# Attention chunks on array quarters: scores and values' products without the masked quarter, in two phases, in a fused gated-attention and expert kernel

## The chip, the cores and the metric

The kernel is one program on one core of a Trainium2 chip. Its time is device time in microseconds (us) from the start to the end of one execution; the time before is the median of three such runs. Beside it stands one execution taken with the hardware profiler. The engines are named as the profile names them: PE is the matrix engine (PEld its weight loads), DVE, ACT and POOL are the three elementwise engines, SP issues most transfers. All data are 32-bit floats; a matmul of the program in that type shows as two passes in the profile's counts (a step's 8 score matmuls are `x16` there), a transpose by the identity as one.

## The reference

Gated linear attention, then a mixture of experts with one expert for each token:

```python
state = np.zeros((B, H, D, D))                       # B=4, H=8, S=768, D=48
for t in range(S):
    state = alpha[:, :, t, :, None] * state + np.einsum('bhd,bhe->bhde', k[:, :, t], v[:, :, t])
    y[:, :, t] = np.einsum('bhd,bhde->bhe', q[:, :, t], state)
x = y.transpose(0, 2, 1, 3).reshape(B * S, H * D)    # 3072 tokens x 384
logits = x @ w_gate + modality_bias[modality_id]     # 8 experts
e = argmax(logits); g = softmax(logits)[e]
out[t] = g * (relu(x[t] @ w1[e]) @ w2[e])            # w1 384x1024, w2 1024x384
```

## The kernel before, in words

**Attention.** A batch's 768 tokens are cut in six chunks of 128, so there are 24 units of work, unit i being chunk i % 6 of batch i // 6, with all 8 heads. Heads go in pairs: pair j holds head 2j on partitions 0 to 47 and head 2j+1 on partitions 64 to 111. For a unit the decays a are turned by PE transposes (`turn_decay`, then two DVE scans in `decay`), k and q are turned and scaled by them (`scale_k`, `scale_q`), and then

- `scores`: kh x qh, 128 keys by 128 queries for each head. ACT copies each of the two results out of PSUM (`scT`), and POOL's affine select sets the entries to zero in which the key lies behind the query.
- `keys`: kh turned back, for the state (`knat`).
- `combine`: one PSUM tile `y` takes three groups of products. U x qh is the state's part of the output (not in a batch's first chunk); kn x v is the state's update (not in the last chunk); v x scT is the chunk's own part. DVE then forms the next state `S` from `y`, and `UB` from it.
- `outputs`, `rows`, `logits_turned`, `logits`: ACT copies y to `yt`, PE turns it into token rows (`xs`, written to DRAM `xd`), and the gate's logits are formed for two units at a time, in every odd step.

The units are pipelined over steps: step s turns the decays of unit s, scales k and q of s-1, does keys and scores of s-2, combine of s-3, outputs and rows of s-4. PE keeps the order in which the program writes its matmuls in steps after the third (`pin`); the other engines' orders come from a scheduler. Step s issues the loads of unit s+2. `guard` is an ACT pass over a unit's decays as they were loaded (`junk`, with a sum `gacc` from which the kernel knows whether a decay is out of range); it stands on ACT ahead of the copy `X` of the same unit's turned decays, and it waits there for the load.

**Experts.** Tokens are ranked by expert and gathered in 12 full slots of 256 tokens and a half slot of 128 (number NS0 = 12). A slot's first layer and second layer each split their operands in a high and a low part and sum three products, `layer1` and `layer2`. `layer2` works for two halves u of 128 tokens; each has a PSUM tile `sc` of its own (two buffers), which ACT scales by the gate into `os`, and POOL scatters `os` to the output (`put`). Before the gather is ready, PE does the first slot's first layer (`first_layer`) with attention steps still running. After the half slot comes a branch on POOL and other engines, on whether more slots are needed; with these inputs none are. The half slot's result is put into `of`, which is scattered behind that branch, at the program's very end.

Of the kernel before, what the change touches and what calls it, by code (L numbers as in the profile page):

```python
# [40 lines left out]
PAD = 32  # L41
# [13 lines left out]
def attention_moe(ctx: ExitStack, tc: tile.TileContext, q, k, v, alpha, mid, wg, mb, w1, w2, out):  # L55
# [12 lines left out]

    def row(i):
        return i * P + (i * P >= MID)  # L70
# [13 lines left out]
    for i in range(NV):  # L84
        t = ac.tile([P, H, 64], F32, name=f"vt{i}")
        VT.append(t)
        pool.memset(t[:, :, D:], 0.0)

# [16 lines left out]
    def first_layer(j, z, name="tr", bufs=3):  # L105

        if z == 0:
            hps.append(ps.tile([P, 2, T], F32, name=name, bufs=bufs))
# [4 lines left out]
    def first_inputs():  # L113
        for d0, d1 in ((0, 2), (2, 3)):
            xp = ps.tile([P, d1 - d0, T], F32, name="sc", bufs=2)
# [23 lines left out]
    for g in range(2):  # L139
        for o in range(2):  # L140
            sp.dma_start(
                wgp[64 * g : 64 * g + D, o::2, :E], wg.rearrange("(a o g d) e -> o g d a e", o=2, g=2, d=D)[o, g ^ o]
            )
# [126 lines left out]

    def scores(i):
        kh, qh = st[i, "k"], st[i, "q"]
        pp = [ps.tile([P, NP, P], F32, name="sc", bufs=2) for _ in range(2)]
        for j in range(NP):
            for g in range(2):
                r = slice(64 * g, 64 * g + D)
                pin(pe.matmul(pp[g][:, j], kh[r, j], qh[r, j], start=True, stop=True))
        st[i, "s"] = []
        for g in range(2):
            s = sb.tile([P, NP, P], F32, name="scT", bufs=4)  # L280
            mark["sc"] = act.copy(s, pp[g])  # L281
            pool.affine_select(s, s, [[0, NP], [1, P]], ALU.is_ge, 0.0, base=0, channel_multiplier=-1)  # L282
            st[i, "s"].append(s)
# [11 lines left out]

    def combine(i):
        c = i % NC
        qh, vt, sc = st[i, "q"], VT[i % NV], st[i, "s"]
        U = UB[i % 2]
        halves = [slice(64 * g, 64 * g + 64) for g in range(2)]  # L300
# [5 lines left out]
        yk = ps.tile([P, 2, 512], F32, name="y")  # L306

        def y(r, j):
            return yk[r, j % 2, P * (j // 2) : P * (j // 2 + 1)]

        kv = yk[:, 1, 2 * P : 2 * P + NP * D].rearrange("p (j d) -> p j d", j=NP)
        fresh = {(o, g) for o in range(2) for g in range(2)}

        def first(o, g):
            new = (o, g) in fresh
            fresh.discard((o, g))
            return new

        if c > 0:
            for a in range(2):  # L320
                for o in range(2):
                    for g in range(2):
                        x, j = g ^ o, 2 * a + o
                        pin(pe.matmul(y(halves[x], j), U[halves[g], j], qh[halves[g], j], start=first(o, x), stop=False))
        if c < NC - 1:
            kn = st[i, "n"]
            for h in range(H):
                j = h // 2
                r = halves[h % 2]
                pin(pe.matmul(kv[r, j], kn[:, j, r], vt[:, h, :D], start=first(1, h % 2), stop=False))  # L330
        for j in range(NP):
            for x, r in enumerate(halves):
                g = x ^ j % 2
                pin(pe.matmul(y(r, j), vt[:, 2 * j + g], sc[g][:, j], start=first(j % 2, x), stop=(j > 1)))
        if c < NC - 1:
            S1 = sb.tile([P, NP, D], F32, name="S")
            if c > 0:
                vec.tensor_tensor(S1, U[:, :, :D], kv, op=ALU.add)
            else:
                vec.tensor_copy(S1, kv)  # L340
# [3 lines left out]
    def outputs(i):  # L344
        yt = sb.tile([P, 2, NP, P], F32, name="yt") if i % 2 == 0 else st[i - 1, "yt"]
        with issue_after("X"):
            act.copy(
# [449 lines left out]
    for s in range(NU + 3):  # L797
# [28 lines left out]
        if s < NU:  # L826
            guard(s)
# [257 lines left out]
```

## Time and profile before

| what | value |
|---|---|
| median of 3 runs | 405.47 us (403.87 to 410.87) |
| profiled execution | 406.9 us, of it a span of 405.2 us |
| mean granted clock of PE in it | 0.983 |
| busy: PE, DVE, ACT, POOL | 378.9, 272.8, 224.1, 136.0 us |
| steady attention steps | 25.6 to 126.2 us of the span, 17 steps |
| end of attention, routing | to about 178 us |
| expert slots | 178 to 398 us |

Times in the profile's rows are counted from the start of the span. A row of the timeline has the start and the length of a run of like instructions on an engine, both in us, then the line of the program, the operation, output and inputs, how much of the array a matmul uses (rows by columns), and, in brackets, how long the engine stood idle before and what ended that. The next run on the same engine may begin before the last has ended, since the engines are pipelined; the distance from start to start is what a run costs.

### The profile page before, as it was taken

How to read it: one execution, taken by the hardware profiler on the slowest of the kernel's cores; microseconds unless marked ns; L12 is line 12 of the kernel's file. 1: busy time of each engine (PE TensorE's matmuls, PEld its weight loads, DVE VectorE, ACT ScalarE, POOL GpSimd, SP SyncE). 2: the span in 40 equal slices, each digit the busy share in tenths (PEclk: the TensorE clock that was granted, in tenths of full speed). 3: DMA queues.
4: the chain of work that ended last, by engine and by line, in shares of the span. 5: the costliest groups of instructions: out<-in, count | busy, mean ns of one | idle time of the engine just before them, and what ended most of it. 6: DMA issues, size and time to landing. Idle time of an engine off the chain costs nothing. (4 is left out here: it accounts for less than half of the span.)

```text
span 405.2 us, 9558 instructions
## 1 busy us (share of the span) xinstructions
PE 378.9 (94%) x3659; PEld 349.0 (86%) x3659; DVE 272.8 (67%) x550; ACT 224.1 (55%) x425; POOL 136.0 (34%) x175
## 2 busy tenths in 40 slices
PE   3898999999999987989997999999999999999992
PEld 3787788888878776779997999999999999999992
DVE  6787889878889962487688566665756666554230
ACT  3467577567665543345586646565554656545230
POOL 9321311321233253302665515344251634222010
PEclk9999999999999997999998999999999999999998
DMA  6999898678764079505999776576867657520010
GB/s 127 202 199 224 195 196 174 149 169 194 152 156 109 21 255 344 183 22 195 387 356 345 250 260 209 201 229 191 278 190 261 212 197 241 147 104 35 6 42 10
DMA packets 132655, 75.12 MB, mean 185 GB/s; under 512 B 103777, under 2 KB 120222, under 8 KB 132600
## 3 DMA queue, kind: packets, MB, share of 16 engines
q1 hardware_dynamic: 128504, 64.57, 56.9%
q0 software_dynamic: 4096, 9.85, 7.1%
q8 instruction: 31, 0.51, 0.5%
q14 instruction: 24, 0.20, 0.1%
HBM read 64.95 MB, written 9.65 MB: 184 GB/s over the span
## 5 line engine op out<-in xcount | busy, mean ns | idle before, releaser
L925 PE MATMUL tr<-xH,w1H 128*128 128x256 f32 x264 | 74.7, 286 | 1.3 <-DVE hL L932 1.3
L926 PE MATMUL tr<-xL,w1H 128*128 128x256 f32 x264 | 75.0, 285 | 0.0
L927 PE MATMUL tr<-xH,w1L 128*128 128x256 f32 x264 | 74.9, 285 | 0.0
L282 POOL TENSOR_SCALAR_AFFINE_SELECT scT<-scT 128x512 f32<-128x512 f32 x48 | 35.6, 763 | 102.3 <-ACT scT L281 102.3
L948 PE MATMUL sc<-w2H,hH 128*128 128x384 f32 x192 | 65.3, 342 | 1.0 <-ACT hH L929 1.0
L949 PE MATMUL sc<-w2L,hH 128*128 128x384 f32 x192 | 64.4, 336 | 0.0
L950 PE MATMUL sc<-w2H,hL 128*128 128x384 f32 x192 | 63.5, 340 | 0.0
L899 DVE TENSOR_TENSOR w2L<-w2r,w2H 128x768 fp32r<-128x768 f32 x52 | 49.1, 957 | 20.5 <-ACT w2H L897 20.3
L899 DVE TENSOR_TENSOR w1L<-w1r,w1H 128x768 fp32r<-128x768 f32 x44 | 41.7, 956 | 21.2 <-ACT w1H L897 20.6
L866 POOL DMA_INDIRECT out_dram<-os,odx x24 | 26.8, 1116 | 83.8 <-ACT os L953 35.6
L897 ACT CAST w1H<-w1r 128x768 fp32r<-128x768 f32 x44 | 36.0, 834 | 29.8 <-PE tr L926 22.9
L925 PEld LDWEIGHTS tr<-xH,w1H 128*128 128x128 f32 x264 | 50.9, 194 | 1.6 <-issue 1.6
L926 PEld LDWEIGHTS tr<-xL,w1H 128*128 128x128 f32 x264 | 51.2, 194 | 0.0
L927 PEld LDWEIGHTS tr<-xH,w1L 128*128 128x128 f32 x264 | 51.0, 194 | 0.0
L679 POOL DMA_INDIRECT xg<-xd,idx x26 | 31.3, 1206 | 50.7 <-PE y L887 41.6
L897 ACT CAST w2H<-w2r 128x768 fp32r<-128x768 f32 x52 | 42.2, 835 | 6.9 <-PE sc L950 6.8
L932 DVE SCALAR_TENSOR_TENSOR hL<-tr,hH 128x512 fp32r<-128x512 f32 x46 | 31.5, 685 | 10.4 <-ACT hH L929 7.9
L948 PEld LDWEIGHTS sc<-w2H,hH 128*128 128x128 f32 x192 | 36.1, 188 | 2.4 <-ACT hH L929 1.2
L684 POOL DMA_INDIRECT gg<-gd,idx x26 | 30.6, 1177 | 17.4 <-DMA gd<-gs 10.1
L949 PEld LDWEIGHTS sc<-w2L,hH 128*128 128x128 f32 x192 | 36.1, 188 | 0.0
L950 PEld LDWEIGHTS sc<-w2H,hL 128*128 128x128 f32 x192 | 36.0, 188 | 0.0
L929 ACT ACTIVATE hH<-tr 128x512 fp32r<-128x512 f32 x46 | 27.3, 593 | 15.3 <-PE tr L927 9.5
(218 smaller groups left out, 702.3 us busy)
## 6 DMA issues: line engine op xcount, KB each, us to landing
w1r<-in_moe_w_dram SPq DMA_DIRECT2D x26, 768.0 KB
w2r<-in_moe_w_dram SPq DMA_DIRECT2D x26, 768.0 KB
nat_a<-in_alpha_dram SPq DMA_DIRECT2D x24, 192.0 KB
nat_k<-in_k_dram SPq DMA_DIRECT2D x24, 192.0 KB
nat_q<-in_q_dram SPq DMA_DIRECT2D x24, 192.0 KB
vt<-in_v_dram SPq DMA_DIRECT2D x24, 192.0 KB
xd<-xs SPq DMA_DIRECT2D x24, 192.0 KB
xg<-xd,idx POOLq DMA_INDIRECT x26
```

Of the source, the lines that this page charges most:

```text
L282: pool.affine_select(s, s, [[0, NP], [1, P]], ALU.is_ge, 0.0, base=0, channel_multiplier=-1)
L679: pool.indirect_dma_start(xg[i % NX][:, u], None, xd[0:rows], ix, bounds_check=rows - 1, oob_is_err=False)
L684: pool.indirect_dma_start(gg[i % NX][:, u : u + 1], None, gd[0:rows], ix, bounds_check=rows - 1, oob_is_err=False)
L897: act.copy(hi, src)
L899: vec.tensor_tensor(lw, src, hi.bitcast(F32), op=ALU.subtract)
L925: pe.matmul(hp[:, z], wH[:, d, fs], xH[:, d], start=(d == 0), stop=False)
L926: pe.matmul(hp[:, z], wH[:, d, fs], xL[:, d], start=False, stop=False)
L927: pe.matmul(hp[:, z], wL[:, d, fs], xH[:, d], start=False, stop=(d == ND - 1))
L932: mark[f"h{j}L"] = vec.scalar_tensor_tensor(hL, hp, 0.0, hH.bitcast(F32), op0=ALU.max, op1=ALU.subtract)
L948: pe.matmul(op, hH[:, z, us], wH[:, z], start=(f == 0), stop=False)
L949: pe.matmul(op, hH[:, z, us], wL[:, z], start=False, stop=False)
L950: pe.matmul(op, hL[:, z, us], wH[:, z], start=False, stop=(f == NF - 1))
```

## The change

1. `scores` does 16 matmuls where there were 8. Each takes 64 keys of one head on a 64x64 quarter of the array. For the second 64 keys only the second 64 queries are computed, since the first 64 are masked (the batch's very first unit computes all, so that the rest of the tile is never unset). The two banks of one lasting PSUM tile `banks` take the results; POOL masks only the 64x64 diagonal blocks, in four selects instead of two of 128x512.
2. `combine` is cut in two phases, as a generator. The state's update and the values' products go 64 keys at a time on quarters, half of them in phase 0, half in phase 1. Between the phases stand the next unit's scores. Phase 1's first matmul waits for a memset of one element on POOL (`tick`), which itself waits for the last matmul of phase 0. Half of the heads' values are needed on the other half of the partitions as well: two POOL copies for each unit (`VS`).
3. `bank(n)` hands out the two halves of `banks` by turns, where a pool of two `sc` tiles was before: in `first_layer`, `first_inputs`, `layer2`, `half`.
4. The half slot's result goes into an ordinary `os`, and its `put` stands in `half`, in front of the last branch; `of` and its memset are not used for it any more.
5. `first_layer(0, ...)` is written around the two phases of step 25's combine, the gate's weights and the copies out of `y` follow the new places of the heads (same sizes), and a filler tile is 24 columns wide instead of 32.

```diff
     def scores(i):
+
         kh, qh = st[i, "k"], st[i, "q"]
-        pp = [ps.tile([P, NP, P], F32, name="sc", bufs=2) for _ in range(2)]
-        for j in range(NP):
-            for g in range(2):
-                r = slice(64 * g, 64 * g + D)
-                pin(pe.matmul(pp[g][:, j], kh[r, j], qh[r, j], start=True, stop=True))
-        st[i, "s"] = []
-        for g in range(2):
-            s = sb.tile([P, NP, P], F32, name="scT", bufs=4)
-            mark["sc"] = act.copy(s, pp[g])
-            pool.affine_select(s, s, [[0, NP], [1, P]], ALU.is_ge, 0.0, base=0, channel_multiplier=-1)
-            st[i, "s"].append(s)
+        pp = banks.rearrange("p g (a o t) -> p g a o t", a=2, o=2)
+        for o in range(2):
+            for z in range(2):
+                for a in range(2):
+                    for g in range(2):
+                        j, r, t = 2 * a + o, slice(64 * g, 64 * g + D), slice(64 * z if i else 0, P)
+                        ins = pe.matmul(pp[halves[z ^ a], g, a, o, t], kh[r, j, halves[z]], qh[r, j, t], start=True, stop=True)
+                        pin(ins)
+        s = sb.tile([P, 2, 2, 2, P], F32, name="scT")
+        for a in range(2):
+            mark["sc"] = act.copy(s[:, a], pp[:, :, a])
+            for b in range(2):
+                m = s[halves[b], a].rearrange("p g o t -> p (g o) t")[:, :, halves[b ^ a]]
+                pool.affine_select(m, m, [[0, 4], [1, 64]], ALU.is_ge, 0.0, base=0, channel_multiplier=-1)
+        st[i, "s"] = s
+        for b in range(2):
+            pool.tensor_copy(VS[i % 2][halves[b], :, :D], VT[i % NV][halves[1 - b], H // 2 :, :D])
...
+        def phase(n):
+            if n:
+                gate.append(chain(pool.memset(tick, 0.0), done[-1], mybir.DependencyClass.Sync))
+            if c > 0 and n == 0:
+                for a in range(2):
+                    for o in range(2):
+                        for g in range(2):
+                            j = 2 * a + o
+                            part(g, o, P * a, P * (a + 1), U[halves[g], j], qh[halves[g], j])
+            if c < NC - 1:
+                kn = st[i, "n"]
+                for a in range(2):
+                    for o in range(2):
+                        for g in range(2):
+                            j, r, lo = 2 * a + o, halves[o ^ n], 2 * P + D * a
+                            part(o, g, lo, lo + D, kn[r, j, halves[g]], vt[r, 2 * j + g, :D])
             for a in range(2):
...
+                for g in (a, 1 - a):
+                    for o in range(2):
+                        r, z = halves[g ^ n], g ^ n ^ a
+                        h = 4 * a + 2 * o + g
+                        v = vs[r, h - H // 2] if a else vt[r, h]
+                        cuts = (0, 64, P) if n and z == 0 and c == 0 else (64 * z, P)
+                        for lo, hi in zip(cuts, cuts[1:]):
+                            last = n == 1 and a == 1 and hi == P
+                            part(g, o, P * a + lo, P * a + hi, v, sc[r, a, g, o, lo:hi], stop=last)
+
+        phase(0)
+        yield
+        phase(1)
...
-            op = ps.tile([P, DM], F32, name="sc", bufs=2)
+            op = bank(DM)
...
-            late = i == NS0 and u == 0
-            os = of if late else mp3.tile([P, DM], F32, name="os", bufs=4)
+            os = mp3.tile([P, DM], F32, name="os", bufs=4)
             act.activation(os, op, AF.Copy, scale=g[:, u : u + 1])
-            if not late:
-                put(i, u, os)
+            put(i, u, os)
...
-        os = of if i == NS0 else mp3.tile([P, DM], F32, name="os", bufs=4)
+        os = mp3.tile([P, DM], F32, name="os", bufs=4)
         act.activation(os, op, AF.Copy, scale=g[:, 0:1])
-        if i != NS0:
-            put(i, 0, os)
+        put(i, 0, os)
...
         tail(NS0)
-    put(NS0, 0, of)
```

**PE, one odd steady step.** Lines have moved with the change: transposes L227 are now L243, rows L357 are L403, scores L277 are L298, the products of `combine` L324, L330 and L334 are all L343. Before, the step's PE order was:

```order
L227 MATMUL tr<-ident,nat_a_94 128x128 x4
L227 MATMUL tr<-ident,nat_k_90 128x128 x4
L227 MATMUL tr<-ident,nat_q_92 128x128 x4
L291 MATMUL tr<-ident,kh 128x128 x4
L369 MATMUL rt<-yt,wgp 32x256 x4
L357 MATMUL tr<-ident,yt 128x128 x4
L277 MATMUL sc<-qh,kh 128x128 x8
L324 MATMUL y<-qh,UB_154 64x128 x8
L330 MATMUL y<-vt_104,knat 64x48 x8
L334 MATMUL y<-scT,vt_104 64x128 x8
```

In a changed step, from the U products on (the three other rows of phase 1's values follow the last one shown):

```order
L343 MATMUL y<-qh,UB_159 64x128 x8
L343 MATMUL y<-vt_109,knat 64x48 x8
L343 MATMUL y<-scT,vt_109 64x128 x2
L343 MATMUL y<-scT,vt_109 64x64 x2
L343 MATMUL y<-scT,vs_113 64x128 x2
L343 MATMUL y<-scT,vs_113 64x64 x2
L298 MATMUL sc<-qh,kh 64x128 x4
L298 MATMUL sc<-qh,kh 64x64 x4
L298 MATMUL sc<-qh,kh 64x128 x4
L298 MATMUL sc<-qh,kh 64x64 x4
L343 MATMUL y<-vt_109,knat 64x48 x8
L343 MATMUL y<-scT,vt_109 64x64 x2
```

The scores have gone from in front of the U products to between the phases, and 32 matmuls have become 56.

**ACT, the same kind of step.** From one copy `yt` to the next, before, with the guard `junk` behind the two copies `xs`:

```order
L347 COPY yt<-y 128x2x2x128
L293 COPY knat<-tr 128x512
L371 COPY lts<-rt 128x256
L361 COPY xs<-tr 128x2x96
L362 COPY xs<-tr 128x2x96
L250 ACTIVATE junk,gacc<-nat_a_94,bhi 128x384
L281 COPY scT<-sc 128x512 x2
L232 COPY X_150<-tr 128x4x128
```

And in the changed kernel (guard L266, knat L318, lts L417, xs L408, scT L302, X L248):

```order
L396 COPY yt<-y 128x512
L266 ACTIVATE junk,gacc<-nat_a_95,bhi 128x384
L318 COPY knat<-tr 128x512
L417 COPY lts<-rt 128x256
L408 COPY xs<-tr 128x4x48 x2
L302 COPY scT<-sc 128x512 x2
L248 COPY X_155<-tr 128x4x128
```

The guard stands behind `yt` directly, ahead of knat, lts, xs, scT and X. It does so in ten of the sixteen steps from step 8 to 23 (10, 11, 14 to 17, 20 to 23); before, it stood behind `yt` in one of these (step 9).

**PE, the second expert slot.** Before, the end of the second layer, its two PSUM tiles sc_3202 and sc_3232 (u = 0 and 1) taken by turns, then the next slot's first layer:

```order
L948 MATMUL sc_3202<-w2H_3162,hH_3158 128x384 [waits Activation_49]
L949 MATMUL sc_3232<-w2L_3137,hH_3131 128x384
L950 MATMUL sc_3232<-w2H_3135,hL_3133 128x384
L948 MATMUL sc_3232<-w2H_3135,hH_3131 128x384
L949 MATMUL sc_3202<-w2L_3164,hH_3158 128x384 [waits DVE_49]
L950 MATMUL sc_3202<-w2H_3162,hL_3160 128x384
```

In the changed kernel, the end of u = 0, three matmuls of the next slot's first layer, and the start of u = 1:

```order
L996 MATMUL sc_71<-w2L_3771,hH_3765 128x384
L997 MATMUL sc_71<-w2H_3769,hL_3767 128x384
L972 MATMUL tr_3883<-xH0_3519,w1H_3867 128x256 [waits Activation_49]
L972 MATMUL tr_3910<-xH0_3519,w1H_3871 128x256 [waits PE_49]
L972 MATMUL tr_3937<-xH0_3519,w1H_3875 128x256 [waits PE_49]
L995 MATMUL sc_71<-w2H_3688,hH_3684 128x384 [waits Activation_49]
```

Both u write the one tile sc_71, and u = 1 starts behind a wait for ACT, whose instruction is the copy `os` of u = 0.

On POOL, the branch L1036 stood ahead of the last scatter L866 of `of`; now the scatter of `os` (L913) stands ahead of the load and branch (L1079, L1080).

More of the change, by code (lines that the diff above doesn't have):

```diff
@@ L39 @@
 NG = 2 * E
-PAD = 32
+PAD = 24
 EARLY = (16, 18)
@@ L67, in attention_moe, with bank @@
     ps = ctx.enter_context(tc.tile_pool(name="ps", bufs=1, space=PSUM))
+    banks = ps.tile([P, 2, 512], F32, name="sc")
+    turn = []
+    def bank(n):
+        turn.append(n)
+        return banks[:, len(turn) % 2, :n]
     def row(i):
@@ L87, in attention_moe @@
         pool.memset(t[:, :, D:], 0.0)
+    VS = []
+    for i in range(2):
+        t = ac.tile([P, NP, 64], F32, name=f"vs{i}")
+        VS.append(t)
+        pool.memset(t[:, :, D:], 0.0)
     WR = [
@@ L294, in keys, with chain @@
             st[i, "n"] = kn
+    tick = cp.tile([1, 1], F32, name="tick")
+    def chain(ins, other, kind):
+        info = mybir.DependencyInfo(kind, mybir.DependencyReason.DATA)
+        tc.add_manual_dep(ins.ins, other.ins.name, info, reason="row tiles")
+        return ins
     def combine(i):
         c = i % NC
-        qh, vt, sc = st[i, "q"], VT[i % NV], st[i, "s"]
+        qh, vt, vs, sc = st[i, "q"], VT[i % NV], VS[i % 2], st[i, "s"]
         U = UB[i % 2]
-        halves = [slice(64 * g, 64 * g + 64) for g in range(2)]
         if c > 0:
@@ L306, in combine @@
         yk = ps.tile([P, 2, 512], F32, name="y")
[L308 to L319, printed above, removed]
-            for a in range(2):
[L321 to L334, printed above, removed]
+        fresh = {(b, x) for b in range(2) for x in range(2)}
@@ new lines, in combine, with part @@
+        done, gate = [], []
+        def part(b, x, lo, hi, *operands, stop=False):
+            ins = pin(pe.matmul(yk[halves[x], b, lo:hi], *operands, start=(b, x) in fresh, stop=stop))
+            fresh.discard((b, x))
+            if done:
+                chain(ins, done[-1], mybir.DependencyClass.NoSync)
+            if gate:
+                chain(ins, gate.pop(), mybir.DependencyClass.Sync)
+            done.append(ins)
+        def phase(n):
[14 more added lines that the diff above has]
+                            part(o, g, lo, lo + D, kn[r, j, halves[g]], vt[r, 2 * j + g, :D])
+            for a in range(2):
+                for g in (a, 1 - a):
[7 more added lines that the diff above has]
+                            part(g, o, P * a + lo, P * a + hi, v, sc[r, a, g, o, lo:hi], stop=last)
@@ L823, in attention_moe @@
             rows(s - 4)
+        steps = combine(s - 3) if 0 <= s - 3 < NU else iter(())
+        if s == NU + 2:
+            first_layer(0, 0, own=True)
+        next(steps, None)
         if 0 <= s - 2 < NU:
             scores(s - 2)
+        if s == NU + 2:
+            first_layer(0, 1)
+        next(steps, None)
         if s < NU:
@@ L847, in attention_moe @@
     outputs(NU - 1)
-    first_layer(1, 0, "sc", 2)
+    first_layer(1, 0, own=True)
     first_layer(1, 1)
```

41 lines of the change are left out of this document (20 added, 21 removed).

## Prediction

> **What bounds the kernel now.** I read the page's head first: which engine has no air, and when.
>
> ```profile
> PE 378.9 (94%) x3659; PEld 349.0 (86%) x3659; DVE 272.8 (67%) x550; ACT 224.1 (55%) x425; POOL 136.0 (34%) x175
> PE   3898999999999987989997999999999999999992
> ```
>
> PE is busy for 94% of the span, with small holes at the start and around slices 15 to 21. So PE's work counts first. But 94% is an average over two programs, attention and experts, and nearly all of the change lies in attention. The busy times by stage (columns: window, its length, then busy time and count for PE, PEld, DVE, ACT, POOL, then granted clock, DMA share, GB/s):
>
> ```profile
> 25.60:126.20 100.60, 98.17 (x1425) 81.84 (x1426) 85.10 (x178) 67.52 (x161) 24.69 (x34) 1.00 0.83 179
> 126.20:137.00 10.80, 10.80 (x161) 8.80 (x160) 10.41 (x27) 6.57 (x15) 3.01 (x4) 1.00 0.21 58
> 137.00:178.00 41.00, 36.35 (x406) 29.25 (x406) 23.41 (x102) 17.45 (x39) 13.66 (x15) 0.92 0.58 199
> ```
>
> The first row is 17 steady steps, 5.92 us each: PE stands for 2.43 us in all, DVE is at 85%, the transfers at 83%. PE bounds these steps, but the next limits are near, at 85.1 and 83.5 us of 100.6. Third, the timeline of PE for one odd step:
>
> ```profile
> 78.41 0.65 PE L227 MATMUL tr<-ident,nat_a 128*128 128x128 f32 x4
> 78.90 0.60 PE L227 MATMUL tr<-ident,nat_k 128*128 128x128 f32 x4
> 79.34 0.60 PE L227 MATMUL tr<-ident,nat_q 128*128 128x128 f32 x4
> 80.23 0.64 PE L369 MATMUL rt<-yt,wgp 128*32 128x256 f32 x8 [0.29 <-ACT yt L347]
> 80.80 0.66 PE L357 MATMUL tr<-ident,yt 128*128 128x128 f32 x4
> 81.39 1.16 PE L277 MATMUL sc<-qh,kh 48*128 48x128 f32 x16
> 82.48 0.67 PE L324 MATMUL y<-qh,UB 64*64 64x128 f32 x16
> 83.07 0.67 PE L330 MATMUL y<-vt,knat 128*64 128x48 f32 x16
> 83.58 1.06 PE L334 MATMUL y<-scT,vt 128*64 128x128 f32 x16
> 84.56 0.33 PE L227 MATMUL tr<-ident,nat_a 128*128 128x128 f32 x1
> ```
>
> From start to start: scores 1.09, U products 0.59, state 0.51, values 0.98, together **3.17 us** of this step's 6.15. These four are what the change rewrites.
>
> **What it saves on PE, step by step.** A 128-column transpose pass costs 0.11 us (78.90 to 79.34, four of them). The 16 U passes on 64x64 quarters run four side by side: four groups of 0.11 make 0.44, and 0.15 is left for the change of array mode at the block's start. The state's 16 passes, 48 columns wide, two side by side, take 0.51/8 = 0.064 us a pair: so a narrow pass has a floor near 0.06 where its columns would ask for 0.11 x 48/128 = 0.04. The changed block, with four quarters side by side:
>
> - U products as now, 0.59.
> - State: twice as many passes (32), eight groups of four at the floor 0.064: 0.51, as now. The other two quarters come free, and the phases halve the keys.
> - Scores: four groups of 128 columns at 0.11 and four of 64 columns at 0.064: 0.70.
> - Values: eight groups. In a group two quarters have 128 columns and two have 64. In lockstep each costs 0.11: 0.88. If quarters run on their own, nearer 0.70.
>
> The sum is 2.68 us; the scores' and values' own changes of mode (about 0.2 and 0.1 in the old rows) fall away, since the whole block stays in one mode. It saves **0.5 us a step**, 0.7 at best.
>
> Nothing on PE's path grows by the new gate, I think. Phase 1's first matmul waits for a one-element memset on POOL, and that for phase 0's last matmul; the 16 score matmuls, 0.70 us, are issued between. A memset of a [128,1] tile is the nearest row; from a matmul's start to the start of what waits for it I take 0.4 us, worked out from the expert stage's rows below (370.38 to 370.75). So 0.4 + 0.09 + about 0.1 for the signal back: 0.6 under a cover of 0.70. The bounds are 0 and, with the cover gone, 0.6 us a step.
>
> ```profile
> L493 POOL MEMSET beg<- 128x1 f32 x1 | 0.1, 88 | 0.0
> L282 POOL TENSOR_SCALAR_AFFINE_SELECT scT<-scT 128x512 f32<-128x512 f32 x34 | 24.7, 749 | 78.2 <-ACT scT L281 78.2
> ```
>
> Behind the memset on POOL stand the next selects and value swaps, and behind those the values' products of the next step. POOL's load goes from two selects of 0.75 us to four smaller selects, two copies and a memset: by the rows between 0.09 and 0.75 each I take 0.4, 0.35 and 0.09, 2.4 us of a step of over 5. POOL idled for 78.2 us on `scT`, so this hides; if selects stayed at 0.75, 3.8 us would still fit, but the scores' masks would come 1.5 us later, still a step ahead of their use.
>
> **What is late next: ACT.** A saved 0.5 us counts only if `yt` is ready for PE sooner. ACT's order decides it. Before, in a step from 84.56 on (the last PE row is the next step's start):
>
> ```profile
> 89.85 0.65 PE L227 MATMUL tr<-ident,nat_a 128*128 128x128 f32 x4
> ...
> 86.59 0.59 ACT L293 COPY knat<-tr 128x512 f32<-128x512 f32 x1 [0.26 <-PE tr L291]
> 87.25 0.32 ACT L361 COPY xs<-tr 128x192 f32<-128x192 f32 x1
> 87.46 0.33 ACT L362 COPY xs<-tr 128x192 f32<-128x192 f32 x1
> 88.87 0.62 ACT L250 ACTIVATE junk<-nat_a,bhi 128x384 f32<-128x384 uint32 x1 [1.08 <-DMA nat_a<-in_alpha_dram]
> 89.48 1.06 ACT L281 COPY scT<-sc 128x512 f32<-128x512 f32 x2
> 90.55 0.58 ACT L232 COPY X<-tr 128x512 f32<-128x512 f32 x1
> 91.03 0.59 ACT L347 COPY yt<-y 128x512 f32<-128x512 f32 x1
> ...
> 92.48 0.37 ACT L371 COPY lts<-rt 128x256 f32<-128x256 f32 x1
> ...
> 93.66 0.62 ACT L250 ACTIVATE junk<-nat_a,bhi 128x384 f32<-128x384 uint32 x1
> ```
>
> The guard `junk` stands idle until its load lands at 88.87, 4.3 us after the step's start. In the next step, which PE begins at 89.85, it starts at 93.66 without a wait, so there the load had landed within 3.8 us. By the order rows the changed kernel puts the guard right behind `yt` in ten of sixteen steps, ahead of knat, lts, xs, scT and X. From the landing on ACT then does guard 0.6, knat 0.55, xs 0.5, scT 1.05, X 0.5 and the next yt 0.6, in odd steps lts 0.3 as well: the next `yt` is done 3.8 or 4.1 us behind the landing, in an even step 7.6 to 8.1 us after its start.
>
> An odd step needs `yt` for L369 1.82 us after its own start (78.41 to 80.23), an even step about 2.0 for L357 (16 turns of a, k, q and kh and two of logits stand ahead, 18 x 0.11). An odd step is 6.15 us in the rows above and the mean 5.92, so an even one is 5.7; with 0.5 less it is 5.2. It offers 5.2 + 1.82 = 7.0 us up to that use, `yt` comes at 7.6 to 8.1, and the odd step waits for 0.6 to 1.1. A pair of steps gains 1.0 on PE and keeps 0 to 0.4 of it. The even step behind has air again: its use comes some 6.15 + 2.0 = 8.15 us after the odd step's start, and `yt` 7.9 at the early landing. I take **0.3 us** for a pair whose even step has the early guard, and the full 1.0 for the others. The ends are 0 and 1.0 for all. That an early wait of ACT does stop PE is in this trace already, where the guard stood right ahead of X:
>
> ```profile
> 43.06 0.62 ACT L250 ACTIVATE junk<-nat_a,bhi 128x384 f32<-128x384 uint32 x1 [1.23 <-DMA nat_a<-in_alpha_dram]
> 45.01 0.64 PE L369 MATMUL rt<-yt,wgp 128*32 128x256 f32 x8 [0.56 <-ACT yt L347]
> ```
>
> Five even steps have an early guard (10, 14, 16, 20, 22); I give them five of the 8.5 pairs.
>
> **Experts and tail.** Both halves u of `layer2` now share one tile, so u = 1 waits for the copy `os` of u = 0:
>
> ```profile
> 370.38 0.33 PE L950 MATMUL sc<-w2H,hL 128*128 128x384 f32 x1
> 370.67 0.28 PE L926 MATMUL tr<-xL,w1H 128*128 128x256 f32 x1
> 370.75 0.58 ACT L953 ACTIVATE os<-sc,gg 128x384 f32<-128x384 f32 x1 [0.16 <-PE sc L950]
> ```
>
> From the last matmul's start to the end of `os` are 0.95 us, 0.78 of them beyond the matmul's own slot of 0.17. The order fills them with 15 or more first-layer matmuls of 0.12 us (370.55 to 370.67 is one) in most slots, 1.8 us: covered. The first slot has only a few short matmuls there, the second three, 0.36 us: about 0.4 and 0.5 us show, **+0.9**. Without any filler it would be 0.8 x 12 = +9.4.
>
> At the end, the last matmul, the half slot's copy and its scatter, and the chain's row that lies between:
>
> ```profile
> 397.57 0.34 PE L993 MATMUL sc<-w2H,hL 128*128 128x384 f32 x1
> 397.95 0.58 ACT L995 ACTIVATE of<-sc,gg 128x384 f32<-128x384 f32 x1 [3.57 <-PE sc L993]
> 401.38 0.98 POOL L866 DMA_INDIRECT out_dram<-of,odx  x1 [11.12 <-ACTq L1036]
> ```
> ```profile
> 398.27 2.88 issue
> ```
>
> `of` is done at 398.53, the scatter starts 2.85 us later, behind POOL's load and branch, and the span ends 3.8 us after that. Moved ahead, the scatter starts at 398.6; POOL's load and branch still follow it: 398.6 + 1.0 + 2.9 = 402.5, and about 1.3 to close (an estimate: of the 3.8 us now, about 2.5 taken for the scatter's landing). The end is then near 403.8: **-1.4 us**, with bounds 0.5 and 2.85.
>
> **The sum**, against the profiled execution of 406.9 (span 405.2 and 1.7 around it): steady steps -(5 x 0.3 + 3.5 x 1.0) = -5.0; two steps in the second window, where PE is busy throughout, -1.0; the other five units, at the start and in the third window, where PE stands for 4.65 of 41 us, half of 5 x 0.5, -1.3; experts +0.9; tail -1.4. Together -7.8, so 399.1. That execution lies 1.4 above the median of the runs shown, 405.47, so I forecast **397.7**.
>
> **A rule of the Trainium skill against the row.** The floor of a narrow pass decides whether narrower pieces pay. The trace has 0.064 us for the state's 48 columns. The Trainium skill, "TensorEngine Tiling (Array Packing)", section Instruction Overhead, says that a matmul on this chip carries some 60 cycles of overhead, that one with a free size of 1 takes as long as one of 60, and that no tiling factor should be taken from a size that is small already. That speaks against 64- and 48-column pieces. At 0.11 us for 128 columns, its 60 columns are an estimate of 0.052 us; the block by that would be 2.68 less 12 x 0.012, some 2.5 us, so the rule, true as far as the state's row shows, still leaves a gain here, because quarters share the floor four at a time.
>
> **The rivals.**
>
> *All of PE's saving shows* (17%). Loads land earlier, or ACT's wait is absorbed: 24 units at 0.5 to 0.7 is 12 to 16.8, with -1.4 and +0.9 a time of 389.6 to 394.4, by the median 388 to 393. For it: ACT has 33 of 100.6 us idle. Against it: DVE's 85.1/17 = 5.0 us a step against the 5.4 then left, and the order rows.
>
> *No gain in attention* (25%). Either the landing moves back as steps shorten (transfers at 0.83 would need 0.9 of the shorter step; at 4.7 us the pair is as long as now), or quarters don't start independently and every pass costs PE some time of its own however narrow. One full-array row bounds that (the tile's view: shortest, median and longest in ns, first and last start in us):
>
> ```profile
> L632 PE MATMUL rt<-OH,OL x24: 177/177/192, 188.4 to 189.0; 128*128 128x34 f16 x24
> ```
>
> Its 24 passes, 34 columns wide, start within 0.6 us, 26 ns apart (22 to 30 by the rounding). The block grows from 64 to 112 passes; at 26 ns they take 2.9 us and 0.15 for the mode, 3.05: a gain of 0.1 a step, at most 2.5 in all. The time is 404 to 406.4, by the median 402.5 to 405.
>
> *Slower, by passes* (7%). If a quarter pass costs what the U row gives in all, 0.59/16 = 37 ns, then 112 of them cost 4.1 us, 1.0 more than now: +24 us less 0.5, a time of 429. It decides from 3.17/112 = 28 ns on. Against it speak the 26 ns, and that 0.15 of the U row is a one-time cost.
>
> *Slower, by the gate* (6%). If POOL answers phase 1 only after two selects of 0.75, in 2.1 us instead of 0.6, PE stands 2.1 - 0.7 = 1.4 in each of 24 steps and saves 0.5: +21.6, with tail and experts a time of 428. It decides from an answer of 1.2 us on, the cover and the saving together. Against it: POOL's order has the memset ahead of the next unit's selects, and POOL is idle most of a step.
>
> *The forecast* (45%) has 394 to 401 as its own range.
>
> **The numbers.** Two per cent of 405.47, about what a measurement of this kernel tells from no change, is 8.1: faster means under 397.4, slower over 413.6. The forecast lies on the bound, and I put 0.28 of its 0.45 below it. Faster: 0.28 + 0.17 = 0.45. Slower: 0.07 and half of the gate's case, 0.10. Same: the rest, 0.45. The range from 389 to 406 takes in the forecast, the no-gain case and most of the full saving; it leaves out both slower cases and a few chances at either end. What could move any case by 3 us is the granted clock, 0.92 in the third window, if its slow stretch falls on other work.
>
> **What the changed profile would show.** PE's block from U products to the next a-turns at 2.6 to 2.8 us, with no idle time named after POOL in front of phase 1; at 3.05 or more the cost is in the passes. The L369 successor (L415) idle for `yt` by 0.6 to 1.1 us in half of the odd steps and nearly never in the others; ACT's `junk` idle for the load right behind `yt`. POOL near 2.4 us a step. u = 1 of `layer2` waiting for `os` in the first two slots alone. The last scatter ahead of the last branch, and the span's end 5.3 us after the half slot's copy. The forecast is wrong if the landing of `nat_a` moves with the steps, if the floor of a narrow quarter pass is not shared by four, or if PE's clock drops where it did not.

## The result, and the profile after

The changed kernel takes **432.94 us** (median of 4 runs, 430.13 to 434.74) beside 408.15 for the kernel before in the same series: a ratio of 1.069, 95% interval 1.058 to 1.080. It is slower by 25 us, where 397.7 was forecast and 406 was the range's upper end. Its profiled execution has a span of 432.0 us beside 405.2.

The page of the changed kernel, its busy times and its row of PE slices:

```profile
PE 377.6 (87%) x4779; PEld 349.2 (81%) x4779; DVE 271.9 (63%) x550; ACT 221.8 (51%) x425; POOL 174.2 (40%) x296
PE   4886888798878784879989799999999999999993
```

PE's busy time has hardly changed (378.9 before), but its share has fallen from 94% to 87%: the time went into waits in the attention half of the slices. The same by stage. The first row is the 17 steady steps of the kernel before, now cut from the a-turns of the sixth unit to those of the 23rd; the others are the changed kernel's: the same 17 steps, the rest of attention, and the first 60 us of the expert slots.

```profile
29.38:130.96 101.58, 99.20 (x1431) 82.33 (x1429) 86.40 (x182) 68.12 (x161) 24.23 (x34) 1.00 0.80 173
```
```profile
30.33:144.51 114.18, 94.34 (x2224) 80.27 (x2221) 86.89 (x183) 65.56 (x161) 59.51 (x119) 0.96 0.71 154
144.51:200.00 55.49, 41.47 (x696) 34.26 (x695) 29.54 (x115) 20.01 (x44) 22.56 (x41) 0.85 0.44 151
200.00:260.00 60.00, 53.77 (x375) 50.80 (x375) 40.83 (x90) 31.73 (x52) 25.47 (x22) 0.97 0.72 247
```

A steady step went from 5.98 to 6.72 us, 12.6 us over the 17. PE stood idle for 2.4 us of them before and for 19.8 now, and the granted clock fell from 1.00 to 0.96. The work itself did get cheaper. The block in an undisturbed step:

```profile
70.08 0.67 PE L343 MATMUL y<-qh,UB 64*64 64x128 f32 x16
70.57 0.40 PE L343 MATMUL y<-vt,knat 64*64 64x48 f32 x16
70.79 0.39 PE L343 MATMUL y<-scT,vt 64*64 64x128 f32 x7
...
71.14 0.85 PE L298 MATMUL sc<-qh,kh 48*64 48x128 f32 x32
71.81 0.40 PE L343 MATMUL y<-vt,knat 64*64 64x48 f32 x16
72.03 0.41 PE L343 MATMUL y<-scT,vt 64*64 64x128 f32 x8
72.17 0.39 PE L343 MATMUL y<-scT,vs 64*64 64x128 f32 x8
72.49 0.66 PE L243 MATMUL tr<-ident,nat_a 128*128 128x128 f32 x4
```

From 70.08 to 72.49 are 2.41 us, beside 3.17 before: 0.76 saved, more than the 0.5 of the forecast. What PE waits for is another matter (us in total over the span, times, longest):

```profile
PE tr L403 <- DVE kh L278: 9.0, 9, 2.3
PE y L343 <- POOL tick L353: 6.9, 2, 6.1
PE tr L403 <- DVE amin L260: 6.6, 5, 2.0
PE tr L316 <- ACT X L248: 6.3, 6, 3.0
```

Before, PE waited for kh once (0.6 us) and for X twice (1.5 us in all). **The rows' transposes (L403) wait for DVE.** Their PSUM tile is one of three that the turned k occupies too, and that is free once DVE has formed kh from it (`amin` is a short operation of DVE on the scan's result, which stands close behind kh in such a step). In the worst step DVE and PE did this:

```profile
80.52 0.94 DVE L523 TENSOR_TENSOR OL<-ioh,lo 128x768 f16<-128x768 f16 x1
81.39 1.43 DVE L256 TENSOR_TENSOR_SCAN G<-X,DR 128x516 f32<-128x516 f32 x1
82.74 0.66 DVE L278 TENSOR_TENSOR kh<-tr,G 128x512 f32<-128x512 f32 x1
```
```profile
83.54 0.63 PE L403 MATMUL tr<-ident,yt 128*128 128x128 f32 x4 [2.31 <-DVE kh L278]
84.10 0.78 PE L343 MATMUL y<-qh,UB 64*64 64x128 f32 x16
88.11 0.33 PE L243 MATMUL tr<-ident,nat_a 128*128 128x128 f32 x1
```

DVE does the scan G of the next unit first and kh behind it. Before, kh stood first in every step from the fourth on; in the changed kernel the scan stands first in 15 of the 19 steps from 5 to 23. And the wait costs more than its 2.31 us: the block that follows takes 4.01 us instead of 2.41, since the clock is down. Two stretches of the same step (columns as in the tables by stage, the granted clock being the third number from the end):

```profile
79.00:84.10 5.10, 2.79 (x29) 2.37 (x26) 5.06 (x14) 1.84 (x5) 3.92 (x6) 1.00 0.70 152
84.10:88.10 4.00, 4.00 (x113) 3.94 (x112) 1.42 (x3) 2.16 (x7) 0.18 (x2) 0.57 0.44 110
```

The Trainium skill, "TensorE: Matmul & The Clock Gate", part 1 on the clock gate, says that the gate passes fewer clock pulses when PE has been little busy. The trace agrees: PE was busy for 2.79 of 5.10 us, and then the granted clock was 0.57. Not every stop had this price. After the stops of PE that ended at 42.11, 122.39 and 173.20, of 2.97, 2.32 and 6.13 us, the clock was 0.69, 0.61 and 0.50 over the next 4 us; after those of 1.2 to 1.9 us that ended at 62.08, 69.53, 108.38 and 191.41 it stayed at 1.00.

**The phase gate waits behind gathers.** Near the end of attention POOL's queue holds this:

```profile
164.95 1.02 POOL L724 DMA_INDIRECT xg<-xd,idx  x1 [0.30 <-issue]
170.72 0.99 POOL L729 DMA_INDIRECT gg<-gd,idx  x1 [4.75 <-DMA gd<-gs]
172.02 1.00 POOL L729 DMA_INDIRECT gg<-gd,idx  x1 [0.30 <-issue]
173.06 0.09 POOL L353 MEMSET tick<- 1x1 f32 x1
```
```profile
173.20 0.68 PE L343 MATMUL y<-vt,knat 64*64 64x48 f32 x16 [6.13 <-POOL tick L353]
```

The memset of 0.09 us stands behind the gathers of the first slots' gates, the first of which waits 4.75 us for a transfer. PE stands for 6.13 us. The next gate that follows gathers, at 191.27, stands behind two of tokens and two of gates (1.87 us of PE).

**ACT waits for loads.** Before, `junk` waited 16.4 us for its load; now

```profile
ACT junk L266 <- DMA nat_a<-in_alpha_dram: 35.0, 19, 3.7
```

The guard that waits there is not that of the unit whose X comes next, as the description of the kernel before has it: counted along ACT's order, the guard of unit 23 stands ahead of the X of unit 20 in both kernels (117.78 and 120.51 us before, 131.00 and 133.25 now).

In sum the span grew by 26.8: 0.9 up to the sixth unit's a-turns, 12.6 in the steady steps, 9.8 from there to the last rows (171.33 before, 194.72 now), 4.2 in the expert slots, and 0.7 less at the end. The expert slots are counted here from the last rows to the start of PE's last matmul.

### The profile page after: what moved, and what is told of

Its sections match the earlier page's. It is cut to its first block, busy times and chain, and to the rows that moved or that the text cites. A ratio compares the mean times of both kernels' runs of the same rounds, so it can differ in the third digit from the quotient of the medians.

```text
span 432.0 us, 11958 instructions
## 1 busy us (share of the span) xinstructions
PE 377.6 (87%) x4779; PEld 349.2 (81%) x4779; DVE 271.9 (63%) x550; ACT 221.8 (51%) x425; POOL 174.2 (40%) x296
## 5 line engine op out<-in xcount | busy, mean ns | idle before, releaser
L974 PE MATMUL tr<-xH,w1L 128*128 128x256 f32 x264 | 73.7, 284 | 0.2 <-issue 0.2
L972 PE MATMUL tr<-xH,w1H 128*128 128x256 f32 x264 | 72.0, 284 | 2.1 <-DVE hL L979 1.7
L995 PE MATMUL sc<-w2H,hH 128*128 128x384 f32 x192 | 66.4, 346 | 2.3 <-ACT hH L976 1.3
L305 POOL TENSOR_SCALAR_AFFINE_SELECT scT<-scT 64x256 f32<-64x256 f32 x96 | 52.3, 545 | 39.2 <-ACT scT L302 33.8
L997 PE MATMUL sc<-w2H,hL 128*128 128x384 f32 x192 | 64.9, 338 | 0.0
L913 POOL DMA_INDIRECT out_dram<-os,odx x25 | 26.0, 1041 | 92.7 <-ACT os L999 59.1
L946 DVE TENSOR_TENSOR w2L<-w2r,w2H 128x768 fp32r<-128x768 f32 x52 | 49.2, 957 | 20.2 <-ACT w2H L944 16.4
L946 DVE TENSOR_TENSOR w1L<-w1r,w1H 128x768 fp32r<-128x768 f32 x44 | 41.5, 954 | 20.9 <-ACT w1H L944 11.7
L972 PEld LDWEIGHTS tr<-xH,w1H 128*128 128x128 f32 x264 | 49.3, 191 | 3.1 <-issue 2.9
L724 POOL DMA_INDIRECT xg<-xd,idx x26 | 27.6, 1062 | 56.9 <-PE y L934 48.4
L256 DVE TENSOR_TENSOR_SCAN G<-X,DR 128x516 f32<-128x516 f32 x24 | 31.7, 1320 | 13.6 <-ACT X L248 13.4
L729 POOL DMA_INDIRECT gg<-gd,idx x26 | 29.4, 1129 | 18.4 <-DMA gd<-gs 11.1
```

The source lines that it names most:

```text
L256: vec.tensor_tensor_scan(G[:, 1:][:, ::-1], x[:, 1:][:, ::-1], DR[:, 1:][:, ::-1], 0.0, op0=ALU.mult, op1=ALU.add)
L305: pool.affine_select(m, m, [[0, 4], [1, 64]], ALU.is_ge, 0.0, base=0, channel_multiplier=-1)
L729: pool.indirect_dma_start(gg[i % NX][:, u : u + 1], None, gd[0:rows], ix, bounds_check=rows - 1, oob_is_err=False)
L946: vec.tensor_tensor(lw, src, hi.bitcast(F32), op=ALU.subtract)
L972: pe.matmul(hp[:, z], wH[:, d, fs], xH[:, d], start=(d == 0), stop=False)
L974: pe.matmul(hp[:, z], wL[:, d, fs], xH[:, d], start=False, stop=(d == ND - 1))
```

## The experiments

All are timed against the kernel before, in series of their own (its medians there: 406.7 to 409.7, and 408.15 beside the changed kernel). A difference in us between runs of two series is uncertain by some 3 us for that reason alone, and the ratios to the kernel before are the better measure. Edits are on the changed kernel unless said.

**DVE's order.** kh ahead of the scan:

```diff
-        vec.tensor_tensor(kh, pk, seg(st[i, "G"][:, 1:], 1), op=ALU.mult)
+        mark["kh"] = vec.tensor_tensor(kh, pk, seg(st[i, "G"][:, 1:], 1), op=ALU.mult)
...
+        with issue_after("kh" if i else None):
             vec.tensor_tensor_scan(G[:, 1:][:, ::-1], ...)
```

> The changed kernel, with one thing added: in every step DVE's scan G of the new decays may only be issued behind the product kh of the unit before, as DVE had it in the kernel before. Theory A (DVE's order): the rows' transposes on PE wait for kh, since kh frees the PSUM tile they need, and kh stands behind a scan of 1.2 to 1.4 us in most steps; then PE's idle time ahead of the rows, 0.35 to 2.3 us a step, goes, with the half-clock stretches that follow it, and the time falls by 10 to 18 us, to 415 to 423. Theory B (guard): yt comes late because ACT waits for the load of the decays, and kh only happens to end then; the time stays within 3 us of 433. Theory C (gate): PE waits for the memset behind gathers on POOL, 8 us in all at the end of attention; this kernel does not touch it, 433.

Measured: 424.39, ratio 1.040 (1.034 to 1.046), 8.6 less than the changed kernel; just short of A's interval. The waits for kh fell from 9.0 to 3.1 us, those named after amin are gone, but X and the gate remain:

```profile
PE y L344 <- POOL tick L354: 11.5, 6, 7.0
PE tr L317 <- ACT X L248: 7.8, 10, 2.3
PE tr L404 <- DVE kh L279: 3.1, 5, 1.2
```

The reverse, on the kernel before: `decay(s)` called ahead of `scale_k(s - 1)`, and kh issued behind the scan.

> The kernel before, with DVE's order turned round: kh stands behind the scan G in every step, nothing else is changed. Theory A: PE's rows wait for kh, in nearly every one of 17 steady steps by 0.3 to 1.2 us, so the kernel before becomes slower by 6 to 18 us, 412 to 426. Theories B and C: nothing on PE hangs on it, within 3 us of 406.

Measured: 410.58 beside 407.43, ratio 1.011 (1.004 to 1.018). The sign is A's, the size half of its smallest. In the trace the 17 steady steps take 106.59 us instead of 101.58. These 5.0 us are close to the 5.9 that kh first takes off the same steps of the changed kernel (108.26 instead of 114.18). So DVE's order is a cause, but not the whole of the 12.6 us. The rows wait here for ACT's knat (3.2 us in these steps) more than for kh itself (1.1).

**POOL's gate.** The second gather of tokens and the gathers of gates behind the last phase gate:

```diff
         early_places(e)
-        gather(e, row(EARLY[e]))
+        if e == 0:
+            gather(e, row(EARLY[e]))
...
-        for e in range(NA):
-            gather_gates(e, row(EARLY[e]))
+        with issue_after("tick"):
+            gather(1, row(EARLY[1]))
+            for e in range(NA):
+                gather_gates(e, row(EARLY[e]))
...
-                at(z + 3, early_gates)
+                at(z + 4, early_gates)
```

> The changed kernel, with the early gather of the second slot's tokens and the two early gathers of gates put on POOL behind the last phase gate instead of in front of the last two. Theory C: the waits of PE for the gate of 6.1 and 1.9 us and the half-clock stretch behind the first go; 8 to 12 us less, 421 to 425. If the gathers' later start is paid for in the first expert slots, up to 4 us of it come back. Theories A and B alone: within 2 us of 433.

Measured: 423.45, ratio 1.042 (1.034 to 1.049), 9.5 less: theory C, a cause by itself. The memset now comes right when it is asked for (163.97, with no idle time ahead of phase 1 there).

**ACT's guard.** First behind the copies scT (`with issue_after("sc" if i > 1 else None):` around it):

> The changed kernel, with the guard on ACT always behind the two copies scT of its step, so that ACT's wait for the load of the decays stands ahead of X alone. Theory B: knat, xs and scT no longer wait for the load, and the steps fall by 0.3 to 0.7 us each, 5 to 12 us in all: 421 to 428. Theory A: kh's place decides, and where X comes no sooner, kh comes no sooner; less than 4 us, 429 to 433.

Measured: 426.44, ratio 1.047 (1.043 to 1.052), 6.5 less, as B had it. Then behind the copy X of its own unit (`issue_after("X" if i else None)`):

> The changed kernel with the guard behind its own X as the only edit. Guard behind scT took 6.5 us off it, and kh first and gathers late with this guard 32. If the three causes add up, the guard's share is 13 us beside 9.5 each of the others: 418 to 422. If DVE's order has to be mended first for the guard to matter, 5 to 8 us as with the guard behind scT: 425 to 428.

Measured: 423.61, ratio 1.042 (1.029 to 1.055), 9.3 less, between the two ranges. With this edit the wait of `junk` for its load is gone from the list of ACT's waits: a unit's own load has landed by then. PE's waits for X are gone too, but those of the rows for DVE are as long as before:

```profile
PE tr L404 <- DVE kh L279: 8.2, 6, 2.3
PE tr L404 <- DVE amin L260: 7.0, 5, 2.0
```

**Two and three at once.** Gathers late and the guard behind X:

> The changed kernel with gathers late and the guard behind its own X, and DVE's order left as the change made it. Theory A holds that kh behind the scan is a cause of its own: 9 to 14 us slower than with kh first, 410 to 415. If the order is only a sign of a late X, which the guard has mended, 401 to 404.

Measured: 414.57, ratio 1.012 (1.006 to 1.018), 18.4 less, where the two alone give 18.8: theory A, kh behind the scan is a cause of its own. kh first and gathers late:

> The changed kernel with both edits at once: kh ahead of the scan G on DVE, and the last early gathers behind the last phase gate on POOL. Each alone took some 9 us off 433. If DVE's order and POOL's gate are two independent causes, the sum: 413 to 417. If both free the same wait (a later gather would have been late anyway), 420 to 424.

Measured: 414.02, ratio 1.020 (1.015 to 1.026): 18.9 less, where the two alone give 8.6 + 9.5 = 18.1: the sum. kh first, gathers late and the guard behind X:

> As the run with both edits, and the guard of a unit stands on ACT behind the copy X of the same unit, when its load has long landed, so that ACT waits for no load. Theory: ACT's 35 us of waits for the load are what is left in front of knat, scT, X and so of the keys on PE; another 5 to 8 us go, 406 to 411. Rival: scT follows the scores, which now end only a microsecond before the block does, and X follows scT, so X stays late whatever the guard does; less than 3 us, 412 to 415.

Measured: **400.70**, ratio 0.986 (0.983 to 0.990), faster than either kernel, and 32.2 less than the changed one; it is called the mended kernel below. The first theory's mechanism holds, and the gain is more than its 5 to 8 us: 13.3 beside the run with the other two edits. By the ratios, kh first, late gathers and the guard take 2.9, 2.8 and 2.8 per cent of the time before off alone, 8.4 in sum, and 8.3 together. So the three add up; that they give more together than alone is not shown. The steady steps, the same 17 as above, first in the kernels with one edit (kh first, the guard), then in the one with all three:

```profile
28.76:137.02 108.26, 92.50 (x2225) 77.91 (x2221) 86.88 (x181) 65.32 (x163) 58.87 (x119) 0.98 0.77 164
```
```profile
27.13:132.88 105.75, 90.62 (x2225) 77.61 (x2221) 88.02 (x181) 65.33 (x161) 58.69 (x119) 0.98 0.80 171
```
```profile
27.55:123.08 95.53, 88.96 (x2224) 76.64 (x2221) 87.48 (x180) 64.79 (x161) 55.49 (x119) 1.00 0.89 190
```

With all three a step takes 5.62 us and the clock is back at 1.00 (the profiled execution, 396.5 us, is the fastest of the five). PE is busy for 88.96 of 95.53 us, DVE for 87.48, and the transfers' share is 0.89; which of them bounds the steps now is not shown. What PE waits for in these 17 steps tells the causes apart (us):

| kernel | 17 steps | rows wait for DVE (kh, amin) | keys wait for X |
|---|---|---|---|
| before | 101.58 | none | 1.1 |
| changed | 114.18 | 11.7 | 6.3 |
| gathers late | 115.79 | 11.1 | 4.9 |
| kh first | 108.26 | 1.3 | 6.7 |
| guard behind X | 105.75 | 11.9 | none |
| all three | 95.53 | 2.5 | none |

kh first takes the rows' wait away and leaves the one for X; the guard's move does the reverse; the gathers touch neither. So kh is not late because of the guard: these are two causes in the same steps, and the gate is the third, behind them.

**Is it the guard and not the change?** The kernel before with the guard behind its own X:

> The kernel before with the guard on ACT behind the copy X of its own unit. If the changed kernel's mended version owes its gain over the kernel before to the guard alone, this one gains as much, 6 us, and stands at 400 to 402. If PE bounds the steady steps of the kernel before, as its 98.2 of 100.6 us say, at most 2.5 us go: 404 to 407.

Measured: 405.70 beside 406.68, ratio 0.997 (0.991 to 1.002). No gain that shows: PE bound those steps. The mended kernel's gain comes from the quarters: in the traces 5.3 us of it lie in the 17 steady steps (100.87 us here, 95.53 there), where kh stands first in both kernels and no gather has begun. Late gathers were not tried on the kernel before.

**X ahead of scT**, on the kernel with all three: the copies and selects of `scores` moved to a function called behind `turn_decay` of the next step, with `issue_after("X")`. The run before it, in the text on record, is the one with all three.

> As the run before it, and the copies scT of a unit's scores stand on ACT behind the copy X of the next step, not ahead of it. If X is late because of the scores' new place late in the block, PE's waits for X ahead of the keys (6 to 8 us in the changed kernel and in the one with kh first) go, and the time falls by 4 to 8 us against the run before it, to 400 to 406. If the masks then come too late for the values' products (four selects of 0.55 us and two copies behind them), it is 2 to 6 us slower than that run.

Measured: 428.25, ratio 1.050 (1.043 to 1.058), 27.6 slower than without this edit, far more than the 2 to 6 of its own rival. PE waits for the masks in nearly every step, and for yt, which now stands behind scT:

```profile
PE y L349 <- POOL scT L311: 13.3, 17, 1.3
PE rt L422 <- ACT yt L403: 8.7, 9, 1.3
```

So the scores' copies stand well where the scheduler had put them.

**The shared tile.** `banks` as two tiles of a bank:

```diff
-    banks = ps.tile([P, 2, 512], F32, name="sc")
+    banks = [ps.tile([P, 512], F32, name=f"sc{g}") for g in range(2)]
...
-        for a in range(2):
-            mark["sc"] = act.copy(s[:, a], pp[:, :, a])
+        for g in range(2):
+            mark["sc"] = act.copy(s[:, :, g], pp[g])
```

> The changed kernel with the one tile banks cut in two tiles of a bank each; the scores' copies go by bank instead of by pair of heads, same sizes. Layer 2's second half need not wait for the copy os of the first any more. If the shared tile costs what was forecast (0.9 us in the first two slots), 431 to 433; if its waits are behind PE's 6.5 us of idle time from 200 to 260 us, 426 to 428. DVE's and ACT's orders stay much as they are, so theory A has nothing to say here.

Measured: 422.61, ratio 1.034 (1.023 to 1.044): 10.3 less, more than either case expected. Of that the expert slots give some 4: from the last rows to the start of PE's last matmul are 226.3 us, beside 230.4 in the changed kernel. The rest lies in attention (111.54 us for the 17 steady steps instead of 114.18), where the scheduler's orders are not the same either. On the mended kernel:

> The kernel with kh first, gathers late and the guard behind its own X (400.7), and the tile banks cut in two tiles as well. Alone on the changed kernel two tiles took some 10 us. If that came from the expert slots' own waits for os, 1 to 4 us more go here, 397 to 400. If it came from attention's chain, which the other edits free already, or from where PE's idle stretches fell, nothing is left: 400 to 402.

Measured: 400.70, ratio 0.987 (0.978 to 0.996), the same as without it. Beside the other three edits, the shared tile costs nothing that shows; why two tiles took 4 us off the slots of the changed kernel stays open.

**The tail alone**, on the kernel before:

> The kernel before with the half slot's scatter in front of the last branch alone. By the forecast's term 1.4 us less (0.5 to 2.85), 404 to 406 beside 407. Rival: the branch's load has to follow the scatter's issue and the landing ends the program either way, less than 0.5.

Measured: 406.39 beside 406.68, ratio 0.999 (0.995 to 1.004): not to be told from nothing by the times. The trace has a gain of 0.7: from the end of the copy to the end of the span were 6.67 us, now 402.2 - 396.24 = 5.96.

```profile
395.66 0.58 ACT L993 ACTIVATE os<-sc,gg 128x384 f32<-128x384 f32 x1 [3.62 <-PE sc L991]
396.52 0.98 POOL L866 DMA_INDIRECT out_dram<-os,odx  x1 [8.60 <-ACT os L993]
```

**POOL beside DVE**, on the kernel with all three edits:

> The kernel with kh first, gathers late and the guard behind its own X (400.7), without POOL's four selects in 22 of 24 units, so those units' scores keep entries of later keys (left out: the masking). If POOL and DVE get in each other's way, DVE's scan G, 1.22 us in the kernel before and 1.33 to 1.34 in the changed one, goes back to 1.22, and since DVE is busy for 87.5 of 95.5 us in the steady steps, 2 to 4 us of the time go: 397 to 399. If the scan is longer for another reason, it stays at 1.34 and the time within 1.5 us of 400.7.

Measured: 459.21, ratio 1.125 (1.113 to 1.137). The whole time says nothing here, since values without masks send tokens to other experts and the slots change; the steady steps can be read. They take 92.3 us for 17 (27.41 to 119.75 by the a-turns) instead of 95.5, and the scan is back at its old length; first its row with the masks, then without:

```profile
L257 DVE TENSOR_TENSOR_SCAN G<-X,DR 128x516 f32<-128x516 f32 x17 | 22.8, 1342 | 0.0
```
```profile
L257 DVE TENSOR_TENSOR_SCAN G<-X,DR 128x516 f32<-128x516 f32 x18 | 22.0, 1223 | 0.0
```

With POOL's selects beside it DVE's scan is longer by 0.12 us in the mean, and with the rest of what they hold up they cost 3.2 us over these steps. Without them no scan G in the steady steps ran beside any work of POOL, so the run does not part the selects from the copies `VS` behind them.

## Why the prediction was wrong, step by step

**What bounds it**: right. PE bound the steady steps, and the guard's move on the kernel before gained nothing, as PE's 98.2 of 100.6 us said.

**The block on PE**: right in kind, too small in size. It saved 0.76 us, not 0.5. The scores took 0.67 (0.70 forecast), the first phase of values 0.35 between starts, where lockstep would have been 0.44 and "on their own" 0.35 (the second, 0.46, holds the block's end as well); the state took 0.22 a phase where 0.064 a group gave 0.26, and the U products 0.49 where they were left at 0.59. Neither the slower rival by passes (37 ns) nor the 26 ns of the no-gain rival holds: 112 passes in 2.41 us are 22 ns each, mode change included.

**"Nothing on PE's path grows by the new gate"**: this is the first step that failed. The memset was compared with the selects beside it. In the steady steps the cover of 0.7 us held but for one wait of 0.78 us. But POOL also issues the early gathers, and two of the last three gates stand behind them, one behind a gather that waits for a transfer. The rival "slower, by the gate" was the right mechanism with the wrong thing in front of the memset; 6.13 and 1.87 us, with the clock after the first, were 9.5 us of the time by the run with late gathers. That the rival's 428 us lies close to the measured time is chance: it had 1.4 us in each of 24 steps, and the gate's cost stood at the end of attention. Of a wait that is added on an engine, all that the engine has in its queue over the program counts, not only what it has in the step at hand.

**"What is late next: ACT"**: this failed too. It followed one engine's order and one tile, `yt`, against the program's old place of everything else. DVE's order had been turned round by the same scheduler, kh behind the scan, and was never looked at; so the tile that PE's rows really waited for, the one that kh frees, was not in the sum: 11.7 us in the 17 steps. The early guard did stand idle for its load, as forecast, but what it held up was X, for which PE waited 6.3 us ahead of the keys, and not `yt`, for which PE waited 0.9 us in three steps. The sum counted on a gain of 5.0 us in these steps, partly eaten by the early guard; they lost 12.6, or 0.74 us a step, and moving the guard alone took 8.4 of it back, kh first alone 5.9. And each of the four stops of 2.3 us or more shown above was followed by PE at 0.50 to 0.69 of its clock, which the forecast mentioned as 3 us either way. By the mean clocks of the spans, (1 - 0.961) x 432.0 = 16.8 us of clock were missing, beside (1 - 0.983) x 405.2 = 6.9 before, and 3.2 in the mended kernel (0.992 of 394.7): an estimate of up to 10 of the 26.8 us.

**"So this hides"** of POOL's added work: half right. Undisturbed, a small select took 0.41 us and a copy 0.34 (the medians), as the sum had them. But some took up to 1.45 us while DVE's scan ran, so POOL was busy for 59.51 / 17 = 3.5 us a step, not 2.4. And DVE's scan went from 1.22 to 1.32 us in the mean.

**Experts +0.9**: 4.2 measured in the changed kernel. The wait for os in the second slot shows as 0.27 us, so the forecast's mechanism is there and small. What makes the rest is not shown: from the last rows to the start of PE's last matmul are 226.2 us before, 230.4 in the changed kernel, 226.8 in the mended one, but 232.6 with the guard's move alone.

**Tail -1.4**: 0.7 to 0.8 in the traces: from the copy's end to the span's end are 5.9 us now, where the sum gave 5.3.

**The range** was not wide enough because both "slower" cases, 13% together, were left out of it, and because no rival stood for a turned order on an engine that was not read.

## What to carry to other kernels

A cheaper block on the busiest engine is worth what the other engines' queues let through: compare the order on every engine that feeds it, before and after, and ask of each PSUM tile it takes what frees it. A gate that is put on a helper engine inherits that engine's whole queue. A loss can have several causes that add up, and then mending any one of them still leaves the change slower; look for all of them before the change is dropped: here each of three edits of order was worth some 2.8 per cent, and together they took the same quarters from 7% slower to 1.4% faster.

## What the hardware showed that was not expected

Four 64x64 quarters take narrow passes side by side at 55 ns for a group (0.22 us for 16 passes of 48 columns), so a pass costs 14 ns, below the 26 ns at which full-array passes of 34 columns, in 16-bit floats, followed each other.

A select on 64 partitions and 256 elements takes 0.41 us in the median, one on 128 partitions and 512 elements 0.63. So half the elements on half the partitions save about a third. The lines give the shortest, the median and the longest in ns, first before, then in the changed kernel:

```profile
L282 POOL TENSOR_SCALAR_AFFINE_SELECT scT<-scT x48: 629/634/1606, 17.0 to 160.2; 128x512 f32<-128x512 f32 x48
```
```profile
L305 POOL TENSOR_SCALAR_AFFINE_SELECT scT<-scT x96: 406/414/1447, 17.6 to 185.6; 64x256 f32<-64x256 f32 x96
L308 POOL COPY vs<-vt x48: 338/343/1367, 11.9 to 176.6; 64x192 f32<-64x192 f32 x48
```

POOL and DVE's scan hold each other up, and the one that starts first has the better of it. In the changed kernel, from 25 to 150 us, ten of 19 scans G took 1.31 to 1.43 us. Each of these began while a select was running that had 0.23 to 0.35 us to go. The nine of 1.22 to 1.23 us began with POOL idle, together with one of its instructions, or with 0.11 us of one left. In turn all 13 selects of over 1 us ran beside a scan G, eleven of them for 1.03 us or more of it. The worst step shows both: the scan began at 81.39 under the last select and took 1.43 us, and the copy that POOL began at 81.80 lasted until after the scan's end at 82.82.

```profile
79.14 2.60 POOL L305 TENSOR_SCALAR_AFFINE_SELECT scT<-scT 64x256 f32<-64x256 f32 x4 [1.21 <-ACT scT L302]
81.80 1.55 POOL L308 COPY vs<-vt 64x192 f32<-64x192 f32 x2
```

The second scan, Fw, stayed at 1.23 us there: it never began with more than 0.17 us of a select to go. In the kernel before, one that did took 1.46. The Trainium skill, "GPSIMD Engine Reference", section Specifications, says that POOL's interfaces to SBUF are shared with DVE and that DVE instructions with two inputs there contend. The scans, with two, agree with it by their 0.1 to 0.2 us.
